# Sharing the low-rank turns of two head pairs, half-row residual products, and masks for the third and fourth pair in an attention and mixer kernel

## The chip, the cores and the metric

The kernel runs on one core of one Trainium2 chip. A core has TensorE (PE, matrix products, with its weight loads shown apart as PEld), VectorE (DVE), ScalarE (ACT), GpSimd (POOL) and SyncE (SP); POOL and SP issue the transfers here. The metric is the device time of one execution in microseconds. Before the change it is 213.51 us, the median of three runs (212.98 to 214.1).

## The reference

Two stages follow each other. The first is an attention over 4 batches, 8 heads, 768 positions and 64 channels, in which a query sees the 96 positions up to its own and the 8 first positions of the sequence, with a bias that falls with the distance. The second is a mixer whose input is the attention's output with the heads side by side (768 x 512 for each batch): a low-rank product along the positions (rank 32), added to its input, and a two-layer network along the channels (512 to 2048 to 512), added again.

```python
scores = scale * np.matmul(q, k.transpose(0, 1, 3, 2))
bias = -slopes[:, None, None] * dist[None, :, :]
scores = scores + bias[None, :, :, :]
scores = np.where(keep, scores, -1000000000.0)
a = np.exp(scores - max);  a = a / (np.sum(a, axis=-1, keepdims=True) + 1e-09)
x = (a @ v) with the heads side by side
h = xt @ U @ V                       # xt: x with positions last; U 768 x 32, V 32 x 768
u = x + h.transpose(0, 2, 1)
ch = np.maximum(u @ w_ch1, 0.0) @ w_ch2
return (u + ch).astype(np.float32)
```

## The kernel before, in words

Work is cut into named tasks. A task names its engine, its instructions, the tasks that it waits for and the buffers that it takes and gives back. A written list, `ORDER`, names all tasks in one order; the class `Planner` walks through it, gives each task a buffer and a planned start from written costs, and sorts the tasks by planned start. Each engine runs its tasks strictly in the order that results. So an instruction can stand behind another of its engine that still waits, although its own inputs are there. Waits themselves are inserted from the data that instructions read and write.

The 8 heads of a batch are taken as 4 pairs, so there are 16 pairs, numbered 0 to 15; a task's number is its pair's, or its batch's in the mixer. One pair goes through these tasks (function `attention`):

- loads of q, k and v (`lq`, `lk`, `lv`, issued by POOL); `TQ` and `TK` turn q and k on PE and `EQ`, `EK` copy the result out of PSUM (pairs 0 to 7), or a transposing transfer on SP does it (pairs 8 to 15); `KO` and `VC`, `VG` are copies of k and v in which the first keys stand in for others.
- `S`: scores on PE in three parts, with 64 rows of the array for each head. `EX`: exponent on ACT. For pairs in `CFG["BI"]`, the distance bias is put into PSUM ahead of the scores by products with a scaled identity (`SB`, line 754). For all others the exponent is multiplied by a mask on DVE (`MK`, lines 847 and 851); the masks come from ACT (line 1391).
- `PV`: weighted sums of v on PE (lines 906, 907). `RC`, `NM`: DVE divides by the sums and writes x in float32 (lines 941, 945). `XC` casts x to 16 bits. For pair 3, the last of batch 0, this runs in three pieces (`PV3.*`, `RC3.*`, `NH3.*`; `NH` writes 16 bits at once, line 925), and `NM3` writes the float32 copy apart.
- The low-rank part. `UP` (line 890): 32 columns, x times U. `XE` (line 996): a copy of them to SBUF, four times side by side. `XU` (line 999): one 128 x 128 product that turns this. `TE` (line 1012): a copy of the turned block to `tmp`, 128 columns for each pair. `HM` (line 1019): products of 32 rows of `tmp` with V, which give the low-rank term of that pair. From pair 4 on, two pairs share one `HM` with four products. `E0`, `E1` make uT, the mixer's input with channels on the partitions: a copy out of PSUM for pairs 0 to 3, where x is turned by identity products in the same banks, or an addition to a turned x which a transposing transfer (`XT`) has brought.

The mixer (function `mlp`) of a batch has a first layer on PE (`M1`, lines 1102 and 1126, and `ZP`, line 1196, a form with seven products in place of eight) with its evacuations on ACT and DVE, and a second layer (`P1` to `P7`, line 1318) in three row tiles. The first thing in each row tile is `RS` (line 1301): four products of 32 rows by 256 columns which put the low-rank term of the output into two banks. It reads `tmp` and `td`, the difference of the halves of `tmp`. DVE adds each finished bank to x in SBUF (`DA` to `DH`), and SP stores the rows (`O`).

Batches overlap: while PE works on the mixer of one, the attention of the next runs in the same lists. Ahead of the first mixer product of batch 0 (`M1a0.*`) stand the attention of pairs 0 to 3 and some of the turns of the next pairs. Where the planner sees PE idle before that, function `idle` puts in products with zeros.

PE takes 128 rows at once in most products, two groups of 64 rows in `S`, and groups of 32 rows in `HM` and `RS`; the code calls these modes 0, 1 and 2.

Of the kernel before, what the change touches and what calls it, by code (L numbers as in the profile page):

```python
# [21 lines left out]
lk0 lq0 wz lq3 ones2 iota Ck0.0 relf bias0 bias1 rel3 Ck0.1 Cq0.1 Cq0.0 TK0 SB0.2 TQ0 SB0.0 mask1 mask6 EQ0.0 EK0.0  # L22
EK0.1 KO0.1 KO0.0 SB0.1 ones1 lk1 TQ3 lq1 ones0 lk3 EQ0.1 S0.1 bias2 bias4 lv0 TK1 S0.0 EX0.1 EQ3 EK1 TQ1 S0.2 EQ1
SB1.1 KO1 TK3 EX0.0 EX0.2 vs1 EK3 SB1.0 VC0 VG0 lk2 lq2 S1.1 EX1.1 S1.0 EX1.0 ones3 lv1 KO3 u16 SB3.1 PV0 RC0 NM0 XC0
lv3 mask4 SB1.2 S1.2 vs0 EX1.2 S3.1 SB3.0 TK2 TQ2 EX3.1 VC1 VG1 EK2 SB3.2 S3.0 EQ2 lv2 EX3.0 VC3 VG3 KO2 S3.2 PV1 RC1
SB2.0 SB2.1 NM1 VC2 EX3.2 S2.1 S2.0 mask0 XC1 EX2.1 PV3.0 PV3.1 PV3.2 EX2.0 RC3.0 SB2.2 RC3.2 S2.2 VG2 NH3.0 UP0 NH3.2
EX2.2 RC3.1 UP1 XE0 XU0 PV2 NM3 NH3.1 RC2 back w1_3 XE1 XU1 TE0 HM0 UP3.0 UP3.1 UP3.2 NM2 XC2 lk4 TE1 HM1 w1_0 lk5 lq4
TK4 TK5 E00 mask3 E01 UP2 M1a0.0 XE3 EK4 XU3 XE2 TE3 TQ4 XU2 TE2 HM3 HM2 KO4 EK5 EQ4 E13 E03 M1c0.0 w1_1 lq6 E02 S4.1
M1a0.1 M1d0.0 M1c0.1 M1d0.1 EX4.1 EX4.2 MK4.1 MK4.2 KO5 mixl vs2 M1b0.0 RL0.0 M1a0.2 M1b0.1 RL0.1 M1b0.6 RM0.6 mask2
M1a0.7 M1c0.2 M1d0.2 M1b0.2 M1a0.6 lq5 TQ5 RL0.7 w1_2 RL0.2 mask5 M1a0.5 lv4 lk6 RL0.6 lv5 VC4 VG4 EQ5 M1b0.7 w1_6  # L30
w1_5 lk7 S4.0 RL0.5 RM0.7 S5.1 w1_4 EX4.0 TK6 M1a0.4 EX5.1 EX5.2 w1_7 M1a0.3 M1c0.3 M1d0.3 M1b0.3 EK6 TQ6 MK4.0 M1b0.5
RL0.4 RM0.5 RL0.3 lq7 ZS1 PV4 MK5.2 w2_1 w2_3 M1b0.4 KO6 RC4 w2_0 M1a0.10 EQ6 NM4 RM0.4 VC5 mask7 S6.0 S5.0 EX6.0
EX5.0 Sa0.0 TD0 Sc0.0 MK5.1 MK5.0 TK7 M1a0.11 M1b0.8 RL0.10 RL0.11 RM0.8 S6.1 EX6.2 M1a0.15 M1a0.14 M1b0.13 M1a0.8
M1b0.10 EK7 EX6.1 XC4 VG5 MK6.1 RL0.15 RL0.8 PV5 M1a0.13 RL0.13 Sb0.0 Sd0.0 M1a0.9 M1a0.12 RL0.14 M1b0.12 KO7 RC5
RL0.9 RM0.10 TQ7 M1b0.15 MK6.2 TWa1 NM5 RL0.12 RM0.12 RM0.13 M1b0.11 EQ7 RM0.11 TWb1 M1b0.14 M1b0.9 RM0.15 S7.1 RM0.14
RM0.9 RS0.0 RS0.2 P10.0 Sa0.1 Sb0.1 EX7.1 EX7.2 P10.2 MK7.1 Sd0.1 S7.0 RS0.1 lq8 w2_2 P20.1 TWa0 DA0.0 lv7 P30.1 DF0.1
MK6.0 MK7.2 TWb0 P10.1 P30.0 P50.1 P20.0 EX7.0 lk8 lv6 lv8 lv9 VC6 Sc0.1 DA0.2 MK7.0 DF0.0 EQ8 VG6 XC5 PV6 EK8 RC6 XT4
UP4 P60.0 P60.2 XE4 VC7 XU4 XT5 P50.2 UP5 lv10 VG7 VC8 XE5 NM6 XC6 KO8 TE4 P20.2 DB0.2 DC0.2 DC0.1 DA0.1 PV7 XU5 RC7
DB0.0 P30.2 UP6 NM7 P50.0 XC7 S8.0 P60.1 P70.0 DF0.2 XE6 EX8.0 TE5 ZS2 HM5 VC10 XU6 TE6 P70.2 DB0.1 UP7 DC0.0 P70.1
E04 DD0.2 E05 DD0.0 lk9 VG10 lk11 lk10 XE7 XU7 TE7 P40.2 HM7 P40.0 XT6 VC9 DD0.1 DG0.2 E06 XT7 DG0.0 ZP11.5 P40.1 E07  # L40
S8.1 E17 M1a1.1 ZT1 EX8.1 EX8.2 ZU1.5 M1b1.1 ZP11.4 RL1.1 M1a1.4 ZP51.4 ZU1.4 RL1.4 M1b1.4 ZP61.5 ZP11.6 ZU1.6 MK8.1
ZS3 ZP61.4 ZP21.6 DG0.1 MK8.0 ZP21.4 ZA1.6 ZP11.7 ZP61.6 RM1.4 ZW1.4 ZA1.4 lq10 lq11 VG9 EK9 KO9 ZP21.5 ZP71.4 ZX1.4
ZW1.6 ZA1.5 ZB1.4 M1b1.5 lq9 ZP51.6 ZP51.5 RM1.5 ZP71.6 ZU1.7 EK10 O0.3 O0.5 ZP31.4 ZX1.6 ZD1.4 ZP21.7 EK11 ZB1.6
ZP61.7 ZP41.6 ZA1.7 ZP41.4 ZP11.2 VG8 O0.1 O0.0 O0.2 ZW1.5 ZP71.5 ZP31.6 O0.4 ZR1.6 EQ9 EQ10 KO11 ZP21.2 KO10 MK8.2
ZU1.2 ZW1.7 ZD1.6 EQ11 ZA1.2 ZP51.7 ZP71.7 ZP61.2 ZR1.4 PV8 ZX1.5 ZP41.5 ZP11.3 ZX1.7 ZB1.5 ZP41.7 ZB1.7 ZP31.7 ZR1.5
RC8 NM8 XC8 lv11 ZP21.3 ZP31.5 ZD1.7 ZW1.2 ZU1.3 S9.0 ZP61.3 ZR1.7 ZP71.2 EX9.0 ZA1.3 ZD1.5 Sa1.1 ZW1.3 ZX1.2 M1a1.5
lk13 lq12 lk12 lv13 RL1.5 lk15 MK9.0 S9.1 ZP51.2 ZP71.3 ZP41.2 Sb1.1 ZP51.3 EX9.2 ZX1.3 ZB1.2 MK9.2 EX9.1 ZB1.3 M1a1.0
M1b1.0 RL1.0 ZR1.2 MK9.1 TD1 ZP31.2 ZP41.3 ZD1.2 ZR1.3 ZP31.3 EK12 PV9 ZD1.3 S11.1 RC9 EX11.1 NM9 RS1.2 P21.2 EX11.2
P11.2 S10.1 RS1.0 EX10.1 EX10.2 P21.0 P11.0 XC9 Sa1.0 XT8 XT9 EQ12 lk14 S10.0 S11.0 EX11.0 Sb1.0 Sd1.1 MK11.2 MK11.1
lq13 DA1.2 EX10.0 VC11 DA1.0 Sd1.0 P61.2 P51.2 P31.2 UP9 UP8 XE8 XE9 MK10.1 P61.0 MK10.2 Sc1.0 MK11.0 XU9 XU8 MK10.0  # L50
P31.0 TE9 DF1.2 DB1.2 DC1.2 PV10 RC10 TE8 VG11 DF1.0 PV11 RC11 NM11 P51.0 NM10 XC11 DB1.0 Sc1.1 XC10 KO12 lv12 RS1.1
P21.1 P51.1 HM9 P31.1 P11.1 E09 lq14 P71.2 lv14 E08 DC1.0 S12.1 DD1.2 P71.0 EX12.1 DC1.1 DF1.1 XT10 DD1.0 DA1.1 MK12.1
P41.2 UP10 UP11 EX12.2 DG1.2 P41.0 XE11 XU11 XE10 XU10 TE11 DG1.0 XT11 TE10 P61.1 HM11 S12.0 DB1.1 EX12.0 VC12 E010
# [18 lines left out]
ZR3.5 ZD3.3 ZP33.5 ZR3.4 ZD3.4 M1b3.5 RM3.5 ZR3.3 ZD3.5 Sa3.3 Sa3.0 Sb3.0 Sa3.1 RS3.0 RS3.1 RS3.2 P13.1 P13.2 P13.0
P23.1 Sd3.0 Sc3.3 Sa3.2 P23.2 DA3.1 P53.2 P53.1 Sb3.3 Sb3.2 DA3.2 Sd3.3 P23.0 Sb3.1 P63.1 P63.2 Sd3.1 Sd3.2 P33.1
Sc3.0 DF3.2 O2.4 DA3.0 Sc3.1 DC3.1 Sc3.2 DC3.2 DB3.1 P63.0 P53.0 DB3.0 DB3.2 P33.0 DC3.0 DF3.0 P73.1 P73.2 DD3.2 DD3.1
O2.3 DF3.1 P73.0 O3.2a DD3.0 P43.2b O2.1 O2.5 O3.0 P43.1 O3.5a O2.0 DG3.2b DG3.1 P43.0 DG3.0 P43.2a O3.1 O3.5c DG3.2a
O3.4 O3.3 O3.5b P33.2 DH3.2 O3.2
# [64 lines left out]
class Planner:  # L141
# [58 lines left out]
    def run(self, names):  # L200
# [5 lines left out]
        mode = 0  # L206
# [1250 lines left out]
```

## Time and profile before

| | us |
|---|---|
| median of three runs | 213.51 |
| the profiled execution, whole | 213.38 |
| its span, first to last instruction | 211.6 |
| around the span | 1.8 |
| PE busy | 204.1 |
| DVE busy | 178.8 |
| ACT busy | 134.1 |
| POOL busy | 74.8 |

PE's busy time is a sum of products that overlap each other, with modelled ends. How long a task holds PE is therefore read from the start of its first product to the start of the next task's first product, in the view of instructions in order of time. For DVE and ACT the durations can be taken as they stand; on DVE an instruction begins up to 0.1 us ahead of the end of the one before it.

### The profile page before, as it was taken

Reading aid. Unit: us, or ns where it says so; the run is one execution under the profiler, and the core shown is the slowest. Engines: PE = TensorE matmul, PEld = TensorE weight load, DVE = VectorE, ACT = ScalarE, POOL = GpSimd, SP = SyncE. Lnnn points to the kernel's source line nnn. Section 1 sums busy time; section 2 is a strip of 40 time slices with the busy share of each in tenths; the row PEclk is TensorE's granted clock in tenths of the full one; section 3 lists DMA queues with packets and bytes.
Section 4 is the critical chain, followed back from the end, with each engine's and each line's share of the span. In section 5 each row is a group of like instructions: output and inputs, shape, how many; then the busy total and the mean of one; then the engine's idle time right before and its main releaser. Section 6 shows DMA issues by size and latency. Waiting matters only on the chain.

```text
span 211.6 us, 5568 instructions
## 1 busy us (share of the span) xinstructions
PE 204.1 (96%) x2240; PEld 146.4 (69%) x2240; DVE 178.8 (85%) x361; ACT 134.1 (63%) x249; POOL 74.8 (35%) x99
## 2 busy tenths in 40 slices
PE   6999899999999999999999999999999999999993
PEld 2555656666699775566797866666879765668892
DVE  4889964989899989899999997859899987677982
ACT  5999799997846638788864465987362347760000
POOL 8997999754008910029466000042000000000000
PEclk9999999999999999999999999999999999999999
DMA  6999999999999999949999977429421302000335
GB/s 185 184 165 168 160 175 177 185 206 192 159 158 101 142 138 274 224 79 133 142 119 167 156 227 170 116 19 120 108 47 50 77 0 99 3 2 3 120 131 196
DMA packets 105545, 27.91 MB, mean 132 GB/s; under 512 B 93104, under 2 KB 102640, under 8 KB 105520
## 3 DMA queue, kind: packets, MB, share of 16 engines
q0 software_dynamic: 72976, 13.78, 82.2%
q1 hardware_dynamic: 32544, 13.78, 31.1%
q8 instruction: 17, 0.28, 0.6%
q14 instruction: 8, 0.07, 0.1%
HBM read 27.75 MB, written 6.29 MB: 161 GB/s over the span
## 4 chain that ended last, share of the span: by engine, by line
PE 78%; DVE 8%; DMA 7%; POOL 4%; issue 1%; ACT 1%; POOLq 0%; DVEq 0%
PE ps L1318 31%; PE ps L1196 18%; PE ps L1102 10%; PE ps L1126 6%; PE ps L773 4%; DMA uT<-x 3%; DMA vt<-in_v_dram 3%; PE ps L907 2%; DVE x_sb L945 2%; PE ps L906 2%; PE ps L1301 2%; POOL stgq L500 1%; PE ps L644 1%; POOL stgk L500 1%; POOL vt L508 1%
## 5 line engine op out<-in xcount | busy, mean ns | idle before, releaser
L838 ACT ACTIVATE ep<-ps 128x1024 f16<-128x1024 f32 (+1 forms) x48 | 43.6, 954 | 14.6 <-PE ps L773 14.3
L1318 PEld LDWEIGHTS <-htr 128*128 128x128 f16 x392 | 36.1, 98 | 6.3 <-issue 2.0
L1330 DVE TENSOR_TENSOR x_sb<-x_sb,ps 128x256 f32<-128x256 f32 (+1 forms) x60 | 26.6, 463 | 4.6 <-PE ps L1318 4.3
L1318 PEld LDWEIGHTS <-sA 128*128 128x128 f16 x288 | 27.1, 98 | 3.5 <-issue 0.2
L1102 PE MATMUL ps<-uT,w 128*128 128x384 f16 x144 | 27.0, 326 | 0.0
L1213 DVE CUSTOM_DVE_ANT_0 htr<-ps,zu 128x384 f16<-128x384 f32 x42 | 21.7, 553 | 6.1 <-PE ps L1196 5.2
L1318 PE MATMUL ps<-w,sA 128*128 128x256 f16 x192 | 24.1, 273 | 0.0
L1318 PE MATMUL ps<-tB,htr 128*128 128x256 f16 (+1 forms) x200 | 23.7, 268 | 0.0
L1318 PE MATMUL ps<-w,htr 128*128 128x256 f16 x192 | 23.6, 273 | 0.0
L409 ACT ACTIVATE zu<-ps 128x384 f32<-128x384 f32 x42 | 19.7, 490 | 5.8 <-PE ps L1196 3.8
L508 POOL DMA_DIRECT2D vt<-in_v_dram x16 | 16.7, 1045 | 15.5 <-ACT xus L409 10.8
L504 POOL DMA_DIRECT2D stgk<-in_k_dram x24 | 19.9, 852 | 5.6 <-DMA kT<-stgk 4.6
L504 POOL DMA_DIRECT2D stgq<-in_q_dram x24 | 19.9, 861 | 0.7 <-PE ps L644 0.4
L1196 PEld LDWEIGHTS <-w 128*128 128x128 f16 x144 | 13.8, 98 | 8.9 <-issue 0.3
L1102 PEld LDWEIGHTS <-w 128*128 128x128 f16 x144 | 13.7, 98 | 8.4
L1108 ACT ACTIVATE htr<-ps 128x384 f16<-128x384 f32 x36 | 16.6, 498 | 3.4 <-PE ps L1102 2.9
L851 DVE TENSOR_TENSOR ep<-ep,mask 128x1024 f16<-128x1024 f16 x24 | 16.1, 682 | 2.4 <-ACT ep L838 2.4
L970 POOL DMA_DIRECT2D x<-x_sb x2 | 1.7, 826 | 44.7 <-PE ps L1102 26.0
L1196 PE MATMUL ps<-uT,w 128*128 128x384 f16 x72 | 16.4, 326 | 0.1
L1196 PE MATMUL ps<-zt,w 128*128 128x384 f16 x72 | 16.5, 326 | 0.0
L945 DVE TENSOR_TENSOR x_sb<-ps,rcp 128x768 f32<-128x768 f32 x16 | 15.1, 951 | 0.6 <-DMA kO<-kT 0.3
L1126 PE MATMUL ps<-uT,w 128*128 128x384 f16 x80 | 15.0, 326 | 0.2 <-DVE uT L1052 0.2
(122 smaller groups left out, 404.1 us busy)
## 6 DMA issues: line engine op xcount, KB each, us to landing
out_dram<-x_sb SPq DMA_DIRECT2D x22, 256.0 KB, 2.3
vt<-in_v_dram POOLq DMA_DIRECT2D x16, 192.0 KB, 5.9
stgk<-in_k_dram POOLq DMA_DIRECT2D x24, 96.0 KB, 5.2
stgq<-in_q_dram POOLq DMA_DIRECT2D x24, 96.0 KB, 5.6
w<-in_moe_w_ch_dram POOLq DMA_DIRECT2D x8, 256.0 KB, 6.5
w<-in_moe_w_ch_dram POOLq DMA_DIRECT2D x4, 512.0 KB, 11.0
stgq<-in_q_dram POOLq DMA_DIRECT2D x3, 192.0 KB, 5.0
stgk<-in_k_dram POOLq DMA_DIRECT2D x3, 192.0 KB, 4.8
```

Source lines behind the costliest of these rows:

```text
L409: nc.scalar.activation(dst, src, AF.Copy)
L504: nc.gpsimd.dma_start(o[:, i], src[b, h0 + i].rearrange("(n p) d -> p n d", p=P))
L508: nc.gpsimd.dma_start(vt[gv.slot][:, :, :, 0:D], v[b, h0:h0 + 2].rearrange("h (n p) d -> p h n d", p=P),)
L838: nc.scalar.activation(ep[gep.slot][:, :, lo:512], ps[:, gsc.slot:gsc.slot + 2, lo:512], AF.Exp, scale=qk_scale)
L945: nc.vector.tensor_tensor(xo, pvo()[:, :, :, 0:D], rcp[p % 2].unsqueeze(3).broadcast_to((P, 2, NB, D)), ALU.mult)
L1102: nc.tensor.matmul(ps[:, g.slot, 0:HS], w1[:, dc, jt * P:(jt + 1) * P], ub[:, dc, i * HS:(i + 1) * HS], start=(dc == 0), stop=(dc == NDC - 1),
L1108: nc.scalar.activation(htr[:, jt, i * HS:(i + 1) * HS], ps[:, g.slot, 0:HS], AF.Relu)
L1126: nc.tensor.matmul(ps[:, g.slot + half, 0:HS], w1[:, dc, jt * P:(jt + 1) * P], ub[:, dc, half * HS:(half + 1) * HS], start=(dc == flat[0]) ...
L1196: nc.tensor.matmul(bank(g), a()[:, i], bq[:, i], start=first and i == 0, stop=last and i == 1, skip_group_check=True,)
L1213: return lambda: nc.vector._custom_dve(TENSOR_ADD_SAT, out=o, in0=x(), in1=y(), s0=3.0e38, s1=0.0)
L1318: nc.tensor.matmul(o if part is None else o[:, part], a[:, j, c0 + cols.start:c0 + cols.stop], bq[:, j] if part is None else bq[:, j, part ...
L1330: nc.vector.tensor_tensor(o, o, x, ALU.add)
```

## The change

Three things change, and the written order and the engines of several copies with them.

1. Two pairs of a batch share one low-rank turn. `UP` of the even pair writes 32 columns and that of the odd pair the next 32 of one bank. One `XE` copies the 64 columns twice side by side, one `XU` turns them and one `TE` copies the result out; `tmp` has 256 columns for a batch in place of 512. One `HM` with four products serves both pairs, in batch 0 too. So there are 8 each of `XE`, `XU`, `TE`, `HM` in place of 16, 16, 16 and 10. Both pairs' `UP` must be done ahead of them.
2. `RS` becomes eight products of 64 rows by 128 columns. Since the 64 rows of `tmp` hold both pairs, V stands in two copies with zeros in the other pair's rows: a fill with zeros (`vz`), and two differences and two copies in `vs2` in place of one difference. `td` is 128 columns wide in place of 256. `RS` has the mode of `S`.
3. Pairs 2 and 3 have no `SB`; their exponents are multiplied by masks (`MK2.*`, `MK3.*`). Six `SB` go, four scaled identities are not made, and six DVE products come.

In the new order the pairs of batch 0 are taken as 0, 1, 2, 3 (before: 0, 1, 3, 2), and the loads follow that. `EQ3` goes from DVE to ACT, `NM3` goes behind `NH3`, `TQ5` goes ahead of the first mixer product. That product is now `M1a0.3` (before: `M1a0.0`), and on PE it stands behind `UP2`, `UP3.*`, `TK5` and `XU3`. The order of the built program has 44 products with zeros ahead of the first mixer product in five places, besides the 8 at the start. The number of masks, loads and stores is the same; of the copies of k and v, `KO` goes by transfers on SP for 2 pairs in place of 3, and `VC` with `VG` for 1 pair in place of 3; ACT and DVE make the others. The last task on PE is `P43.0` (before: `P33.2`), and the last store is `O3.3`, 256 KB, which waits for `DG3.0` (before: `O3.2`, 128 KB, which waits for `DH3.2`).

```diff
-    "BI": [0, 1, 2, 3],
+    "BI": (0, 1),
-    "H2": [4, 6, 8, 10, 12, 14],
-    "R2": {0: (), 1: (), 2: (), 3: ()},
...
-    tmp = sb("tmp", [P, DM], FP16, 2)
+    tmp = sb("tmp", [P, 2 * P], FP16, 2)
-    td = sb("td", [P, hd], FP16)
+    td = sb("td", [P, P], FP16)
...
+    c_vz = add(DVE, 0.55, lambda: nc.vector.memset(vs[:, 1:3], 0.0), name="vz")
...
-                nc.vector.tensor_tensor(o, vf[:, 0:HS], vf[:, HS:S], ALU.subtract)
+                    nc.vector.tensor_tensor(vs[r, 1 + i], vf[r, 0:HS], vf[r, HS:S], ALU.subtract)
+                    nc.vector.tensor_copy(vs[r2, 1 + i], vs[r2, 0])
...
                     nc.tensor.matmul(
-                        low(0, R), xx[:, c], u16[:, c],
-                        start=turned and c == 0, stop=(c == NB - 1), skip_group_check=True,
+                        low(k * R, (k + 1) * R), xx[:, c], u16[:, c],
+                        start=leads and c == 0, stop=(c == NB - 1), skip_group_check=True,
                     )
...
+            def xuevac():
+                copy(
+                    ENG[CFG["XE"][p]], xus[gxu.slot].rearrange("p (g x) r -> p g (x r)", g=2),
+                    low(0, 2 * R).unsqueeze(1).broadcast_to((P, 2, 2 * R)),
+                )
...
+            XE = add(ENG[CFG["XE"][p]], 0.28, xuevac, [f_[-1], l_[-1]], acq=[gxu], name=f"XE{p}")
+            XU = add(PE, 0.06, xuturn, [XE], lat=0.3, rel=[gxu], name=f"XU{p}")
...
+            def hboth():
+                other()
+                hmix()
...
-            nc.vector.tensor_tensor(td, tb[:, hd:DM], tb[:, 0:hd], ALU.subtract)
+            nc.vector.tensor_tensor(td, tb[:, P:2 * P], tb[:, 0:P], ALU.subtract)
...
-                    for n, g, m in ((1, gX, td if i else tb[:, 0:hd]), (2, gY, tb[:, i * hd:(i + 1) * hd])):
-                        r = slice(VR[n] + k * R, VR[n] + (k + 1) * R)
-                        yield half(g, i), vs[r, n, cols], m[r], i == 0
+                    for k in range(2):
+                        for r, g, m in ((slice(64, P), gX, td if i else tb[:, 0:P]), (slice(0, 64), gY, tb[:, i * P:(i + 1) * P])):
+                            nc.tensor.matmul(
+                                half(g, i)[:, k * P:(k + 1) * P], vs[r, 1 + k, cols], m[r], start=i == 0 and k == 0, stop=False, skip_group_check=True,
+                            )
+            RS = add(PE, 0.23, rest, [TD] + mm1_done[b][-1:] + c_vs, lat=0.3, acq=[gX, gY], mode=1, name=f"RS{b}.{t}")
```

More of the change, by code (lines that the diff above doesn't have):

```diff
@@ L21 @@
 ORDER = """
[L22 to L41, printed above, removed]
@@ L72 @@
[L72 to L76, printed above, removed]
+wz lk0 lq0 lk1 iota relf rel3 bias1 bias0 bias2 Ck0.0 mask5 mask7 Ck0.1 Cq0.1 Cq0.0 TK0 lq1 SB0.2 lk2 ones1 EK0.0
@@ new lines @@
+EK0.1 vz ones0 TQ0 SB0.0 lv0 KO0.1 KO0.0 EQ0.1 SB0.1 EQ0.0 mask6 lq2 TK1 S0.0 S0.1 TQ1 EK1 KO1 EQ1 VC0 EX0.0 EX0.1 vs0
+S0.2 SB1.1 TK2 SB1.2 S1.1 S1.2 lv1 TQ2 EK2 ones2 EX0.2 mask4 EX1.2 lk3 lq3 ones3 u16 lv2 VG0 EX1.1 SB1.0 S1.0 KO2 EQ2
+PV0 S2.2 EX1.0 VC1 TK3 VG1 S2.1 lq5 w1_1 EX2.2 lv3 vs1 PV1 lk4 RC0 TQ3 w1_6 NM0 XC0 MK2.2 lk5 w1_0 EK3 EX2.1 RC1 S2.0
+KO3 EQ3 EX2.0 NM1 MK2.1 S3.0 S3.2 VC2 MK2.0 VG2 S3.1 EX3.0 UP0 TQ5 XC1 EX3.1 PV2 MK3.0 MK3.1 VC3 EX3.2 EQ5 UP1 XE1 XU1
+mask0 back TE1 HM1 MK3.2 E00 RC2 VG3 E01 NM2 PV3.0 XC2 PV3.1 PV3.2 RC3.1 RC3.0 RC3.2 NH3.0 NH3.1 mixl TK4 UP2 UP3.0
@@ new lines @@
+NH3.2 EK4 NM3 UP3.1 UP3.2 TK5 lk6 w1_5 lq4 w1_7 XE3 XU3 TE3 EK5 M1a0.3 KO5 w1_4 w2_2 lk7 lv4 w1_3 HM3 M1a0.2 M1c0.2
+M1c0.3 E13 E02 w2_0 mask1 E03 KO4 M1a0.1 M1c0.1 M1d0.2 S5.0 M1d0.3 M1b0.2 mask2 EX5.0 M1d0.1 M1b0.3 M1b0.1 M1b0.13
+M1a0.12 RL0.2 lv5 RL0.3 RL0.1 mask3 S5.1 lq6 M1a0.11 M1b0.14 EX5.1 w1_2 lq7 M1a0.13 TQ4 EX5.2 RM0.14 RL0.11 TK6 w2_1
+w2_3 RM0.13 RL0.12 RL0.13 MK5.1 MK5.2 EQ4 EK6 M1b0.12 RM0.12 M1a0.14 RL0.14 M1b0.10 S4.1 RM0.10 S4.0 M1b0.11 EX4.0
+M1a0.8 RM0.11 EX4.2 M1b0.15 M1a0.9 EX4.1 RL0.8 M1a0.15 M1a0.0 vs2 TK7 ZS2 MK4.2 TD0 EK7 MK5.0 MK4.0 VC4 MK4.1 M1a0.10
@@ L77 @@
+DF3.2 Sd3.1 P63.2 DA3.0 Sd3.3 P33.2 P53.0 P33.1 DC3.1 DB3.1 DC3.2 DH3.2 DB3.2 O3.2a O2.3 O2.2 DF3.1 DC3.0 O2.0 O2.5
+O3.1 O2.4 O2.1 P73.2 P73.1 P63.0 DD3.2 DD3.1 DB3.0 P33.0 P43.1 P43.2a P73.0 DF3.0 DG3.1 DG3.2a DD3.0 P43.2b DG3.2b
+O3.5a O3.0 O3.2 O3.4 O3.5b O3.5c P43.0 DG3.0 O3.3
 """.split()
@@ L206, in run @@
         mode = 0
-        dma_free = {POOL: 0.0, SP: 0.0}
+        dma_free = {POOL: 0.0}
         shared_port = {POOL: [], DVE: []}
@@ L276, in run @@
                 if t.eng == SP:
-                    behind = max(0.0, dma_free[POOL] - s - 0.8)
-                    begin = max(s + t.lead, dma_free[SP])
-                    dma_free[POOL] = max(dma_free[POOL], begin) + need
-                    dma_free[SP] = begin + need
-                    t.end = begin + need + min(0.7 * behind, 6.0) + (1.1 if late else 0.3)
+                    behind = max(0.0, dma_free[POOL] - s)
+                    dma_free[POOL] = max(dma_free[POOL], s + t.lead - 0.8) + need
+                    t.end = s + t.lead + min(0.8 * behind, 6.5) + (0.4 if late else 0.1)
                     clock[SP] += min(0.08 * behind, 0.6)
@@ L583 @@
             add(
-                POOL if vq else DVE, 1.1 if vq else 0.55, build_vs(g), [] if vq else [c_mixl],
+                POOL if vq else DVE, 1.1 if vq else 1.5, build_vs(g), [] if vq else [c_mixl, c_vz, c_vs[1]],
                 size=0.3 if vq else 0.0, parts=2 if vq else 1, fast=0, name=f"vs{g}",
@@ L608 @@
     nm_done, waiting, later = {}, {}, {}
-    m2_done, kept, zt_read, plain_mm, rs_done, rs_of = {}, {}, [], {}, {}, {}
+    m2_done, kept, zt_read, plain_mm, rs_done, ups, shared = {}, {}, [], {}, {}, {}, {}
     def attention(p):
@@ L978, in attention @@
             UP = add(
-                PE, 0.16 if turned else 0.49, mixed(range(NB)), [XC, c_u16], lat=0.3, acq=[gu], rel=[gx16],
+                PE, 0.16 if turned else 0.49, mixed(range(NB)), [XC, c_u16], lat=0.3, acq=[gu] if turned else [gu, gx], rel=[gx16],
                 name=f"UP{p}",
@@ L1009, in attention, with hmix @@
             XT = []
-        def tevac():
-            copy(ENG[CFG["TE"][p]], tmp[b % 2][:, hp * P:(hp + 1) * P], low(P, 2 * P))
-        TE = add(ENG[CFG["TE"][p]], 0.29 if CFG["TE"][p] == "D" else 0.3, tevac, [UP] + xw, rel=[gu] if turned else [], name=f"TE{p}")
-        def hmix(k=0, gx=gx):
+        def hmix(gx=gx):
             for half in (0, 1):
@@ L1057, in evacs, with low_copy, low_add @@
                 ut_done[p] = tuple(ee)
+            elif p in CFG["EA"]:
+                gh = Group("zu")
+                def low_copy():
+                    nc.scalar.activation(
+                        zu[gh.slot].bitcast(FP16).rearrange("p (h c) -> p h c", h=2), ps[:, gx.slot:gx.slot + 2, 0:HS], AF.Copy
+                    )
+                def low_add():
+                    o = uT[b % 2][:, hp]
+                    nc.vector.tensor_tensor(o, o, zu[gh.slot].bitcast(FP16), ALU.add)
+                AH = add(ACT, 0.81, low_copy, [HM], acq=[gh], rel=[gx], name=f"AH{p}")
+                ut_done[p] = (add(DVE, 0.555, low_add, [AH] + w + XT, rel=[gh], fast=2, name=f"E0{p}"),)
             else:
@@ L1068, in evacs @@
                 ut_done[p] = (add(e, 0.81 if e == ACT else 0.95, ev, [HM] + w + XT, rel=[gx], name=f"E0{p}"),)
-        if duo and p % 2 == 0:
+        if k == 0:
             later[p] = evacs
         else:
-            if duo:
-                later[p - 1](HM)
+            later[p - 1](HM)
             evacs(HM)
```

188 lines of the change are left out of this document (90 added, 98 removed).

## The prediction

> **What bounds the kernel now.** I read the page's head first, then the chain of work that ended last in order of time, then two stretches of the view of stages.
>
> ```profile
> span 211.6 us, 5568 instructions
> PE 204.1 (96%) x2240; PEld 146.4 (69%) x2240; DVE 178.8 (85%) x361; ACT 134.1 (63%) x249; POOL 74.8 (35%) x99
> PE   6999899999999999999999999999999999999993
> ```
>
> ```profile
> 17.41 0.34 DVE vo L411
> ...
> 24.59 1.01 DVE x L411
> ...
> 26.29 0.33 PE ps L1126 x2
> ...
> 38.81 0.34 PE ps L644 x6
> ...
> 57.28 0.32 PE ps L1301 x4
> ...
> 70.74 7.29 DMA uT<-x
> ...
> 189.13 0.54 PE ps L1301 x12
> 189.68 18.48 PE ps L1318 x176
> 208.18 0.42 DVE x_sb L1330
> ```
>
> ```profile
> 2.60:25.60 23.00, 20.21 (x343) 12.73 (x341) 20.50 (x54) 20.10 (x35) 21.75 (x31) 1.00 1.79 185
> 26.10:208.20 182.10, 181.73 (x1888) 132.59 (x1884) 157.47 (x307) 112.61 (x213) 50.89 (x60) 1.00 1.08 126
> ```
>
> The columns of the last two rows are the stretch, PE, PEld, DVE, ACT and POOL busy, clock, transfers. The chain has two parts with different limits. From 17.4 us to the cast of pair 2's x, which ends at 24.59 + 1.01 = 25.6 us, it runs on DVE. The first main product (first layer, batch 0) follows at 26.3 us. From there to 208.2 us PE is busy for 181.7 of 182.1 us. The chain leaves PE for a transfer at 70.74 us, but PE has other products meanwhile. So the end is the start of the first main product, plus PE's work behind it, plus the tail: last addition and store, 211.6 - 208.2 = 3.4 us. What the change saves on PE ahead of 26.3 us counts only if that start comes earlier; what it saves behind counts in full while PE isn't made to wait.
>
> **The early part.** PE loses six bias tasks; DVE gains six mask products.
>
> ```profile
> 12.08 0.60 PE L754 MATMUL ps<-rel,ibe 128*128 128x512 f16 x2
> 12.52 0.23 PE L907 MATMUL ps<-vt,ep 128*128 128x65 f16 x2
> ...
> 80.28 0.81 PE L1102 MATMUL ps<-uT,w 128*128 128x384 f16 x4
> 80.93 0.49 PE L1196 MATMUL ps<-zt,w 128*128 128x384 f16 x2
> ```
>
> ```profile
> L851 DVE TENSOR_TENSOR ep<-ep,mask 128x1024 f16<-128x1024 f16 x24 | 16.1, 682 | 2.4 <-ACT ep L838 2.4
> L847 DVE TENSOR_TENSOR ep<-ep,mask 128x768 f16<-128x768 f16 x12 | 6.5, 552 | 1.9 <-ACT ep L838 1.9
> L411 DVE COPY vo<-vt 128x660 f16<-128x660 f16 x7 | 2.9, 413 | 0.4 <-DMA vt<-in_v_dram 0.4
> ```
>
> ```profile
> 6.66 0.56 DVE L411 COPY qT<-ps 128x384 f16<-128x384 f16 x1 [0.60 <-PE ps L644]
> ...
> 7.95 0.96 DVE L411 COPY qT<-ps 128x768 f16<-128x768 f16 x1 [0.29 <-PE ps L625]
> ...
> 13.39 0.23 DVE L941 RECIPROCAL rcp<-ps 128x12 f32<-128x12 f32 x1 [0.95 <-PE ps L907]
> ...
> 21.98 0.25 DVE L411 CAST xus<-ps 128x128 f16<-128x128 f32 x1
> 22.16 0.93 DVE L945 TENSOR_TENSOR x_sb<-ps,rcp 128x768 f32<-128x768 f32 x1
> ```
>
> Two bias products of 512 columns hold PE for 12.52 - 12.08 = 0.44 us, and four of 384 columns take 0.65, so two 0.33. PE is rid of 4 x 0.44 + 2 x 0.33 = 2.4 us.
>
> On DVE, four masks of 682 ns and two of 552 ns come: 3.83 us. Away go `EQ3` (0.96, the row at 7.95, now on ACT), `XE0` (0.25, at 21.98) and, behind the needed pieces, `NM3` (0.93, at 22.16): 2.14 us. The fill `vz` has no row of its shape; it lies between 0 and the 0.41 us of the 660-wide copy. I take 0, since it stands where DVE waited 0.60 us for the first turned q; without that wait it would cost the 0.4. Net: +1.7 us of DVE work ahead of the last piece that PE needs, now `NH3.2`.
>
> DVE was busy for 20.5 of 23.0 us there, so 2.5 us were waits. If the new list fills all of them, `NH3.2` ends at 25.6 + 1.7 - 2.5 = 24.8 us; if none, at 27.3. I take the middle: the waits for first turns (0.60 and 0.29) hang on loads that come no earlier, and the smaller ones stay. The 0.95 us for pair 0's weighted sums is filled, because copies of pair 2 (`EK2`, `KO2`, `EQ2`) now stand before that reciprocal. 25.6 + 1.7 - 0.95 = 26.3 us. Before, the first main product came 0.7 us behind the cast; now `XE3` and `XU3` stand between as well (0.25 and 0.06), but fewer `UP` products are left: 0.8 us. So 27.1 in place of 26.3: **+0.8 us** (bounds -0.7 and +1.8).
>
> **Behind the first main product.**
>
> ```profile
> 53.99 0.23 PE L773 MATMUL ps<-qT,kO 64*128 64x128 f16 x2
> 54.06 0.22 PE L773 MATMUL ps<-qT,kT 64*128 64x128 f16 x2
> ...
> 65.35 0.22 PE L999 MATMUL ps<-ident,xus 128*128 128x128 f16 x1
> 65.41 1.04 PE L1318 MATMUL ps<-w,sA 128*128 128x256 f16 x8
> 66.28 0.30 PE L890 MATMUL ps<-u,x 128*128 128x32 f16 x6
> ...
> 69.05 1.03 PE L1318 MATMUL ps<-w,sA 128*128 128x256 f16 x8
> 70.02 0.23 PE L773 MATMUL ps<-qT,kT 64*128 64x128 f16 x2
> ...
> 72.14 0.34 PE L1019 MATMUL ps<-vs,tmp 32*128 32x384 f16 x4
> 72.42 0.23 PE L999 MATMUL ps<-ident,xus 128*128 128x128 f16 x1
> ```
>
> - `XU`: 65.41 - 65.35 = 0.06 us each; seven of the eight that go stand here: -0.4.
> - Mode changes: the same eight products take 0.87 us ahead of a 128-row product (65.41 to 66.28) and 0.97 ahead of a 64-row one (69.05 to 70.02), so a change costs 0.1. PE's order has 63 behind the first main product before and 59 after, since 9 of the 12 `RS` now stand beside scores of their own mode: -0.4.
> - `HM`: one with four products holds PE for 0.28 us with a change, 0.17 without. `HM2` and `HM3` were two; their products become four that run side by side: -0.17.
> - `RS`: alone 0.32 us with a change, 0.22 without; the three of the last batch took 0.54 together. Two products of 64 rows by 128 columns go every 0.06 us in the scores (53.99 to 54.06), so eight take 0.24 us. 12 x 0.24 against 9 x 0.22 + 0.44: about +0.4. If the two halves didn't run side by side it would be twice 0.24, +2.9 more; the scores speak against it.
> - `TQ5`, 0.34 us (the row at 38.81), is done ahead: -0.34.
>
> Together **-0.9 us**. At nothing I cost: 7 copies to `xus` and 7 to `tmp` less on ACT, busy for 134 of 211.6 us; the two more differences and the two copies of `vs2`, which lie while PE has first-layer products (cover gone: about 1 us); three fewer SP copies; the narrower `td`.
>
> **The tail.**
>
> ```profile
> out_dram<-x_sb SPq DMA_DIRECT2D x22, 256.0 KB, 2.3
> ...
> out_dram<-x_sb SPq DMA_DIRECT2D x3, 128.0 KB, 1.7
> ```
>
> The last store is now 256 KB in place of 128: +0.6 us. And `P43.0` waits for `DD3.0`, which waits for `P73.0`: 0.17 us until the end of a product is out (1.04 against 0.87 above) and 0.42 of addition, against half a product task (0.44) between them: +0.2. Together **+0.8 us**, with bounds 0 and 1.
>
> **Sum.** 0.8 - 0.9 + 0.8 = +0.7 us on the profiled execution's own 213.38 us (span 211.6 and 1.8 around it): 214.1 us. That execution lies 0.13 us under the median, well inside the runs' spread, so I leave 214.1 us. About 0.5% (1.1 us) is what a measurement of this kernel can tell from no change, so this is no change: 212.4 to 214.6 us.
>
> **The rivals.**
>
> *PE bounds the early part too (faster).* Then its start moves with its work: -2.4 - 0.9 + 0.8 = -2.5, 210.9 us. For it: PE is busy for 20.2 of 23 us there. Against it: the chain lies on DVE, and the new order holds 44 products with zeros there, places that have no work for PE. 0.08. A milder form is likelier: DVE's waits are all filled (-0.7) and the tail costs nothing, -1.6: 211.8 us, 0.14.
>
> *DVE becomes the bound outright (slower).* The masks stand in DVE's line ahead of `XC1`, `NM2`, `XC2` and `NH3`; a mask that waits for its exponent on ACT, busy 20.1 of 23 us there, holds all of these, and so `UP3` and the first main product. None of the 2.5 us filled gives +1.8 - 0.9 + 0.8 = +1.7, 215.1 us; one exponent late by 1 us more, 216.1. It decides once `NH3.2` ends later than 26.7 us. 0.28, at 215.3 us.
>
> *A shared turn comes too late in a later batch (slower).* The even pair's turn now waits for the odd pair. Where the chain runs through the transfer at 70.74 us, there was nothing to spare; 1.5 us there gives 215.6. Against it: PE has second-layer products to go on with. 0.06.
>
> *The half-row products don't do what is said:* 214.1 + 2.9 = 217.0 us; 0.02.
>
> *The masks hold up the loads (slower).*
>
> ```profile
> 29.59 1.53 POOL L554 DMA_DIRECT2D w<-in_moe_w_ch_dram  x2
> ...
> 29.64 0.69 DVE L851 TENSOR_TENSOR ep<-ep,mask 128x1024 f16<-128x1024 f16 x1 [1.56 <-ACT ep L838]
> ...
> L554 POOL DMA_DIRECT2D w<-in_moe_w_ch_dram x8 | 6.2, 793 | 0.7 <-DMA u<-in_moe_U_dram 0.7
> ```
>
> POOL issues nearly all loads early. If each mask kept POOL from issuing for its length, v of pair 3 would come 3.8 us later: 217 us. But two issues took 1.53 us while a mask ran, and eight have a mean of 793 ns, so none was held: 0.02. [...]
>
> **How the numbers follow.** Forecast, no change: 0.40, at 214.1 us. Faster: 0.08 + 0.14 = 0.22. Slower: 0.28 + 0.06 + 0.02 + 0.02 = 0.38. The range goes from 211.7 us, just under the milder faster case, to 216.1, the late exponent; about 0.1 lies beyond each end. The forecast's own range is 212.4 to 214.6.
>
> **What would show it.** The first main product at 27.1 us; `NH3.2` at 26.3; DVE without a wait near 0.95 us around 13 us; PE's stretch from that product to its last one 181.0 us in place of 181.9; a wait of about 0.2 us ahead of the last product task; the last store landing 0.6 us later behind its addition. It is wrong if the first main product comes before 25.9 or after 27.6 us, or if PE waits for over 1 us in sum between 30 and 200 us for a copy of uT.

## The result

The first four executions of the changed kernel gave 214.63, 214.71, 216.94 and 221.67 us, beside 213.26 us for the kernel before in the same session: a ratio of 1.010 (95% interval 1.0061 to 1.0138). Twelve more, among the experiments below, gave 213.87 us in the median (212.6 to 217.5) against 213.23 us: a ratio of 1.0023 (0.9999 to 1.0047). Over all sixteen the middle is 214.2 us; the prediction was 214.1. So by the larger set the change makes no difference that can be measured, and by the first four it is slower by 1%. The spread between executions is itself a result: 35 executions of the kernel before in that last session lay between 212.54 and 214.27 us. The ratios leave out executions over 1.5% above a kernel's fastest, of which the changed kernel has several and the kernel before next to none.

The profiled execution took 214.63 us (before: 213.38), with a span of 212.9 (211.6). The head of its page:

```profile
span 212.9 us, 5699 instructions
PE 205.9 (97%) x2312; PEld 149.6 (70%) x2312; DVE 181.6 (85%) x368; ACT 133.6 (63%) x241; POOL 75.0 (35%) x99
```

The chain that ended last, in order of time, around the first main product and at the end (start, length, engine, tile and line):

```profile
24.36 0.87 DVE x_sb L946
25.23 0.02 issue
25.25 0.94 DVE x L408
26.19 0.05 issue
26.24 0.23 PE ps L887
...
28.21 0.23 PE ps L1020
28.44 0.42 PE ps L1140 x2
...
207.56 0.43 DVE x_sb L1328
207.99 0.04 issue
208.03 1.05 PE ps L1316 x8
209.08 0.02 issue
209.11 0.42 DVE x_sb L1328
```

The first main product (line 1140) comes at 28.44 us, 2.15 later than before. DVE's last addition begins at 209.11 in place of 208.18. From one to the other it is 180.67 us in place of 181.89, so 1.22 us are won there. From the last addition's start to the end of the span it is 3.75 us in place of 3.42, so 0.33 are lost. 2.15 - 1.22 + 0.33 = 1.26 us, which is the difference of the spans (1.3 as printed). The chain begins a piece where the one before it ends; the first main product itself starts at 28.37 us here and at 26.14 before, and below these starts are given. The view of stages for the same two stretches (columns as before):

```profile
2.60:27.45 24.85, 22.78 (x382) 15.56 (x380) 22.27 (x59) 20.83 (x34) 22.42 (x33) 1.00 1.69 178
28.40:209.10 180.70, 180.52 (x1917) 132.78 (x1915) 157.90 (x308) 111.24 (x205) 50.07 (x59) 1.00 1.05 124
```

Behind the first main product PE is still never idle for long (180.52 of 180.70 us). So the question is the 2.15 us ahead of it. The first turn of k shows where they begin. In the view of instructions in order of time, before and after:

```profile
5.13 0.49 PE L644 MATMUL ps<-ident,stgk 128*128 128x128 f16 x6 [1.02 <-DVE stgk L411]
```

```profile
5.40 0.80 PE L643 MATMUL ps<-ident,stgk 128*128 128x128 f16 x6 [0.91 <-DVE stgk L408]
```

Six equal products took 0.49 us before and 0.80 after. The trace's records of the granted clock agree: the first record, of the full clock, begins at 3.58 us in the profile of before and at 8.83 us in that of after. (The views print a clock of 1.00 for a stretch ahead of the first record too; the slow products show that it wasn't.) A second profile of the same program, below, has the same row at the same time with the clock from 4.91 us:

```profile
5.40 0.49 PE L643 MATMUL ps<-ident,stgk 128*128 128x128 f16 x6 [0.92 <-DVE stgk L408]
```

DVE's waits up to 25.6 us in the first profile (sum, times, longest):

```profile
DVE kT L408 <- PE ps L624: 1.4, 1, 1.4
DVE stgq L408 <- DMA sA<-in_q_dram: 0.9, 1, 0.9
```

The first line is the wait for the turned k of pair 1, 0.7 us in the second profile: here DVE pays for the late turns. The second line is not the clock's work. Pair 0's q landed 4.9 us after its issue here, against 3.7 in the second profile. It is a rival for the late start, but PE was busy without a break from 5.42 to 8.83 us (3.41 of 3.41 us), so the turns waited for PE and not for that q.

### The profile page after: what moved, and what is told of

Its sections match the earlier page's. It is cut to its first block, busy times and chain, and to the rows that moved or that the text cites. A ratio compares the mean times of both kernels' runs of the same rounds, so it can differ in the third digit from the quotient of the medians.

```text
span 212.9 us, 5699 instructions
## 1 busy us (share of the span) xinstructions
PE 205.9 (97%) x2312; PEld 149.6 (70%) x2312; DVE 181.6 (85%) x368; ACT 133.6 (63%) x241; POOL 75.0 (35%) x99
## 4 chain that ended last, share of the span: by engine, by line
PE 87%; DVE 9%; issue 1%; POOL 1%; ACT 0%; POOLq 0%; DVEq 0%
PE ps L1316 35%; PE ps L1210 19%; PE ps L1116 11%; PE ps L1140 6%; PE ps L772 5%; PE ps L908 2%; PE ps L907 2%; PE ps L643 2%; PE ps L1305 1%; DVE x_sb L946 1%; DVE vo L408 1%; PE ps L753 1%; PE ps L891 1%; PE ps L1002 1%; DVE x L408 1%
## 5 line engine op out<-in xcount | busy, mean ns | idle before, releaser
L1328 DVE TENSOR_TENSOR x_sb<-x_sb,ps 128x256 f32<-128x256 f32 (+1 forms) x60 | 27.1, 462 | 4.9 <-PE ps L1316 4.2
L1116 PE MATMUL ps<-uT,w 128*128 128x384 f16 x144 | 26.2, 326 | 0.0
L850 DVE TENSOR_TENSOR ep<-ep,mask 128x1024 f16<-128x1024 f16 x28 | 18.9, 684 | 6.4 <-ACT ep L837 6.4
L1316 PE MATMUL ps<-tB,htr 128*128 128x256 f16 (+1 forms) x200 | 24.2, 268 | 0.1
L1210 PE MATMUL ps<-uT,w 128*128 128x384 f16 x72 | 16.0, 326 | 0.0
L1140 PE MATMUL ps<-uT,w 128*128 128x384 f16 x80 | 15.1, 326 | 0.0
```

The source lines that it names most:

```text
L850: nc.vector.tensor_tensor(ev, ev, mv, ALU.mult)
L1116: nc.tensor.matmul(ps[:, g.slot, 0:HS], w1[:, dc, jt * P:(jt + 1) * P], ub[:, dc, i * HS:(i + 1) * HS], start=(dc == 0), stop=(dc == NDC - 1),
L1140: nc.tensor.matmul(ps[:, g.slot + half, 0:HS], w1[:, dc, jt * P:(jt + 1) * P], ub[:, dc, half * HS:(half + 1) * HS], start=(dc == flat[0]) ...
L1210: nc.tensor.matmul(bank(g), a()[:, i], bq[:, i], start=first and i == 0, stop=last and i == 1, skip_group_check=True,)
L1316: nc.tensor.matmul(o if part is None else o[:, part], a[:, j, c0 + cols.start:c0 + cols.stop], bq[:, j] if part is None else bq[:, j, part ...
L1328: nc.vector.tensor_tensor(o, o, x, ALU.add)
```

## The experiments

Theory C: the late full clock makes the first turns late and so the first main product; its price is 1.2 us. Theory D, its rival: DVE's longer list, the 3.8 us of masks above all, sets the start whatever the clock does. (C, D, T and Q are only names for what an experiment sets out to tell apart.) Where nothing else is said, the kernels compute all that the reference does.

**More zeros at the start, and fewer**

```diff
 # after
-                    idle(int(gap / 0.43), 512, bank)
+                    idle(int(gap / 0.43) + 3, 512, bank)
```

> The changed kernel with 11 products with zeros at the start in place of 8. Theory C (clock at the start): in the changed kernel's profile PE stood without work from 4.5 to 5.4 us and its full clock was granted only at 8.8 us (before: 3.6), which moved every first turn and the first main product by 1.2 us. With PE busy until about 5.5 us the clock is granted by then, the first main product comes at 27.2 us in place of 28.4, and the time is 213.4 us. Rival D (DVE's list alone is late): the clock changes nothing that counts, first main product at 28.4 us, 214.6 us.

Measured: 214.72 us (ten executions), ratio 1.0057 (1.0039 to 1.0075). In its profile the full clock came at 6.40 us and the first main product at 27.37, 1.0 us earlier than in the profile of after; but the span was again 212.9. Neither theory had that. The gain was lost in one place, in the list of PE's waits between 150 and 160 us:

```profile
PE ps L772 <- DMA qT<-stgq: 0.9, 1, 0.9
```

These are the scores of pair 13 (`S13.1`), which wait for its turned q. They start at 154.40 us in both profiles; in that of after PE came there no earlier and found q ready. The load `lq13` is the last of three that POOL issues behind `XC12`, here at 143 us; the transposing transfer on SP waits for it.

The counterpart, on the kernel before:

```diff
 # before
-                    idle(int(gap / 0.43), 512, bank)
+                    idle(3, 512, bank)
```

> The kernel before with 3 products with zeros at the start in place of 8. Theory C: PE stands idle from about 2.1 to 5.1 us, the full clock comes only at about 8.5 us in every run, the first turns are later by 1.2 us and the time is 214.6 us. Rival (when the clock comes is chance and no matter of these products): within 0.3 us of the kernel before.

Measured: 214.33 us, ratio 1.0042 (1.0021 to 1.0064). The full clock came at 10.29 us, the first main product at 27.40 in place of 26.14, and the span was 212.7 in place of 211.6. So C's mechanism is real: in the kernel before, 6.7 us more without the full clock moved the first main product by 1.3 us and the span by 1.1.

**Bias products back**

```diff
 # after
-    "BI": (0, 1),
+    "BI": (0, 1, 2, 3),
 # ORDER: bias4 made behind bias2; SB2.*, SB3.* each ahead of its S; MK2.*, MK3.* out
 # each task's buffer held to that of after; the planner then sets 18 small zeros in place of 44
```

> The changed kernel with bias products for pairs 2 and 3 again (six SB in, six masks out), all else in its order and its PSUM banks. Theory D: DVE's line is the limit ahead of the first main product; 3.8 us of masks less bring it forward by 1.5 to 2 us although PE has 2.4 us more work, to about 26.5 us with an early clock and 27.5 with a late one; 212.7 to 213.7 us. Theory C alone: the masks cost nothing, PE has 2.4 us more to do, 214.6 us or more.

Measured: 214.38 us (213.81 to 217.6), ratio 1.0058 (1.0023 to 1.0093). The profiled execution got the full clock at 9.94 us and its first main product at 29.64. With eleven zeros besides:

```diff
 # after, with the bias products back as above
-                    idle(int(gap / 0.43), 512, bank)
+                    idle(int(gap / 0.43) + 3, 512, bank)
```

> The kernel after with TensorE's bias products back for pairs 2 and 3 (no masks for them) and with eleven zero products at the start in place of eight. If the late grant of the full clock makes the spread of the run with the bias products alone (213.8 to 216.3), the times should now stand together at 213.3 to 213.9 us. If the start of the first main product is set by DVE's list and not by the masks or the clock, 214.2 or more.

Measured: ratio 1.0074 (1.0041 to 1.0107); full clock at 5.83 us, first main product at 27.84. Eleven zeros did not hold the times together (214.03 to 218.32), so a late clock at the start is not shown to be what spreads them. D falls in this order of tasks: without the masks the first main product comes later, not earlier. The order was not made for bias products, so what they would cost in one of their own is not shown. Which engine is full is seen in the stages 5 to 10 and 10 to 25 us, of this kernel and then of the kernel after in its second profiled execution (below), where the full clock came at 4.91 us:

```profile
5.00:10.00 5.00, 5.00 (x70) 2.94 (x70) 3.60 (x10) 4.84 (x11) 5.00 (x10) 1.00 1.56 177
10.00:25.00 15.00, 14.32 (x262) 9.21 (x263) 11.17 (x25) 12.73 (x19) 14.99 (x19) 1.00 1.95 176
```

```profile
5.00:10.00 5.00, 4.60 (x78) 3.01 (x78) 3.95 (x12) 4.88 (x11) 5.00 (x10) 1.00 1.59 178
10.00:25.00 15.00, 13.91 (x297) 11.02 (x291) 14.62 (x35) 13.93 (x20) 15.00 (x19) 1.00 1.97 174
```

With bias products DVE has work for 11.17 of 15 us and PE for 14.32; with masks DVE for 14.62 and PE, zeros included, for 13.91.

**Only the masks, on the kernel before**

```diff
 # before
-    "BI": [0, 1, 2, 3],
+    "BI": [0, 1],
 # ORDER: SB2.*, SB3.*, bias4 out; masks made earlier on ACT; MK3.*, MK2.* behind their EX
```

> The kernel before with masks in place of bias products for pairs 2 and 3, and nothing else but the order of the eight masks on ACT. Theory D: 3.8 us more on DVE ahead of the first main product, of which about 1 to 2 us are hidden in its waits: first main product at 28 to 29 us, 215 to 216 us. Rival (PE bounds the early part): 2.4 us less on PE, 211 to 213.4 us.

Measured: 218.0 us, ratio 1.0208 (1.0173 to 1.0243), worse than both. The view of stages shows why; the third number from the end of a row is the granted clock:

```profile
18.00:21.33 3.33, 0.80 (x22) 0.63 (x23) 3.24 (x9) 2.33 (x4) 3.33 (x5) 1.00 1.97 173
21.33:24.74 3.41, 3.41 (x52) 3.12 (x48) 2.58 (x8) 0.81 (x2) 3.41 (x5) 0.50 1.96 159
```

PE stood mostly idle from 18 to 21.33 us (0.80 us of work), and for the next 3.41 us it got half the clock. Theory T: such a stretch follows whenever PE idles enough. To test it, zeros were put where PE had stood idle:

```diff
 # before with masks, as above
+            if t.name in ("S2.1", "PV3.0"):
+                bank = pl.unused("ps", t.start - 0.01, t.start)
+                idle(32 if t.name == "S2.1" else 16, P, bank)
```

> The kernel before with masks for pairs 2 and 3 (218.0 us, half clock from 21.33 to 24.74 us), and with 32 zero products of 128 columns ahead of S2.1 and 16 ahead of PV3.0, where TensorE stood idle for 2.2 and 1.2 us. Theory T: with TensorE busy there the clock stays full, the first main product comes at about 28.5 us in place of 30.5, and the time is 215 to 216.5 us. The rival: half clock as before, 218.

Measured: 216.59 us, and the clock stayed full:

```profile
18.00:21.33 3.33, 3.31 (x66) 3.12 (x64) 3.24 (x10) 2.19 (x4) 3.02 (x4) 1.00 1.94 174
21.33:24.74 3.41, 2.67 (x64) 2.38 (x60) 3.29 (x10) 1.74 (x3) 3.41 (x5) 1.00 1.82 133
```

The first main product came at 29.30 in place of 30.46 us. T holds here. What is left, 29.30 against 26.14, was not taken apart further: it is the masks together with an order that was not made for them.

**Without the 44 small zeros**

```diff
 # after
-                elif bank is not None and gap > 0.15:
+                elif False:
```

> The kernel after without the 44 zero products of 128 columns ahead of the first main product (the eight of 512 columns at the start stay). Theory T: idle TensorE in the early part makes the clock fall to half for a stretch of about 3.4 us, as in the run of before with the masks, at 21.3 to 24.7 us. Then such stretches come in most runs, and the time is 216 to 222 us with a mean granted clock of 0.984 to 0.992. The rival, that the grant depends on something else than TensorE's idle time: 214.6 us, as after.

Measured: 214.66 us (212.97 to 219.78), ratio 1.0056 (1.0019 to 1.0092). One execution in ten had a mean clock of 0.990, the others 0.995 to 1.0; with these zeros three of sixteen had 0.992 or less. So the strong form of T, that these zeros keep the clock up, falls. In the profile the full clock came at 3.89 us and the first main product at 25.82. But PE then waited 1.0 us for pair 13's q again, and 0.3 in another place; the span was 212.0.

**The load of pair 13's q, and the tail**

```diff
 # after, tail: ORDER
-P33.0 P43.1 P43.2a P73.0 ... P43.2b ... P43.0 DG3.0 O3.3
+P33.0 P73.0 ... P43.1 ... P43.0 ... DG3.0 P43.2a ... O3.3 P43.2b O3.5b DG3.2b O3.5c
```

> The kernel after with the last eight product tasks in another order: P73.0 two places earlier, P43.0 behind P43.1, and the two half tasks P43.2a and P43.2b last, so that the last store is 64 KB in place of 256 KB and P43.0 has another task between itself and P73.0. The theory that the tail costs 0.37 us for its larger last store and 0.16 us for the wait of P43.0: both are won back, and some of a smaller store still, 0.5 to 0.9 us under the kernel after, so 213.7 to 214.1 us where after's two even runs gave 214.63 and 214.71. The rival, that the store's landing time doesn't depend on its size there and the wait only moves: no difference, 214.6.

Measured: 214.91 us (212.4 to 217.6), ratio 1.0029 (1.0003 to 1.0054). In the profile the end lay 3.27 us behind PE's last product in place of 3.79, so 0.52 are won. The wait ahead of `P43.0` is gone too, but the last half task, `P43.2b`, now waits for the addition of the other half:

```profile
207.97 0.61 PE L1263 MATMUL ps<-tB,htr 128*128 128x128 f16 x8 [0.38 <-DVE x_sb L1294]
```

Read from start to start, `P43.0` came 0.23 us late in the kernel after and `P43.2b` comes 0.54 late here. That leaves a net gain of about 0.2 us, less than expected and too small to be seen in the times. This profile too lost 0.9 us to pair 13's q.

Theory Q: that load is what the earlier start runs into.

```diff
 # after with eleven zeros: ORDER
-XC12 lv13 ... lv15 ... lq13
+lq13 XC12 lv13 ... lv15
```

> The kernel after with eleven zero products at the start (as the run that gave 214.17 to 214.9 us and lost 0.9 us to the turned q of pair 13 at 154 us), and with the load lq13 issued ahead of XC12, lv13 and lv15 in POOL's line. Theory Q: with an early first main product, that q, whose load is the last of three issued together near 143 us, sets a new bound, and what the early part wins is lost there. Then no wait for it is left, and the time is 213.3 to 213.9 us. The rival, that another wait takes its place or the loads behind it come late instead: 214.2 to 214.9, as without it.

Measured: 213.11 us (ten executions, nine of them 212.6 to 214.24, one 217.47), ratio 0.9991 (0.9974 to 1.0009). Without the early load the same kernel had 1.0057 (1.0039 to 1.0075). PE had no listed wait between 30 and 205 us, and the span was 211.5. Theory Q holds.

> The same, with the last product tasks in the order that puts the two half tasks last (last store 64 KB). The two gains add if each is on the path: 212.7 to 213.4 us in undisturbed executions, about the time of the kernel before or 0.2% under it. If the tail's gain is a wait that only moves: 213.3 to 213.9.

Measured: 213.53 us (212.38 to 218.46), ratio 1.0000 (0.9982 to 1.0017), so the tail added nothing that could be seen in the times. Its chain shows the same wait of `P43.2b`, whose eight products start when the addition ahead of them has ended:

```profile
207.50 0.30 DVE x_sb L1294
207.80 0.04 issue
207.84 0.62 PE ps L1263 x8
208.46 0.02 issue
208.49 0.29 DVE x_sb L1294
```

The same with eight zeros at the start and without the small ones:

> The kernel after with lq13 early and the half tasks last, with eight zero products at the start and without the 44 small ones. From the run without the small ones (first main product at 25.8 us where the full clock came at 3.9 us; it lost 1.0 us to pair 13's q): 212.0 to 212.8 us where the clock comes early, 0.2 to 0.5% under the kernel before; where it comes late, 0.5 us more for each us of delay, up to 215.

Measured: ratio 1.0015 (0.9986 to 1.0043). The profiled execution took 211.98 us (span 210.1, full clock at 4.44 us, first main product at 25.59), the shortest of all; but the times spread from there to 217.0, so the median gains nothing. No version beat the kernel before by more than can be measured.

**The kernel after again**

> The kernel after, unchanged, timed in more executions. If the late grant of the full clock is a matter of chance from execution to execution, its times spread from about 213.4 us (early grant, less the wait for pair 13's q) to over 216; if it comes from the kernel, they stand near 214.7.

Measured: the 213.87 us and the ratio of 1.0023 given above. The times spread as for a matter of chance. The profiled execution, of 217.39 us, had the full clock at 4.91 us and its first main product at 26.67, 1.7 us earlier than in the other profile of the same program: with DVE's list the same in both, this decides against D as it was put. But it still ended 2.7 us later, so this long execution does not come from a late start. Its waits on DVE and on PE between 88 and 104 us, and its stages:

```profile
DVE x_sb L946 <- DMA out_dram<-x_sb: 3.3, 1, 3.3
```

```profile
PE ps L1116 <- DVE x_sb L946: 2.7, 1, 2.7
```

```profile
97.00:99.70 2.70, 0.04 (x1) 0.00 (x0) 0.99 (x2) 0.00 (x1) 2.70 (x4) 1.00 1.87 126
100.48:103.90 3.42, 3.42 (x19) 1.50 (x18) 1.84 (x4) 1.91 (x5) 3.42 (x6) 0.50 2.39 152
103.90:110.00 6.10, 6.10 (x92) 5.07 (x90) 6.07 (x8) 5.14 (x6) 2.77 (x4) 1.00 2.16 169
```

`NM9` must write x where the store `O0.3` still reads. That store stands in SP's line behind six transposing transfers and stores; `EK11` there went at 88.34 us, behind a load that POOL had issued at the same 78.79 us as in the other profile. So `O0.3` left at 93.97 (92.57 in the other profile) and landed 4.6 us later, `NM9` waited 3.3 us, all of DVE's list behind it waited too, PE ran dry at 97.0, and half the clock for 3.4 us followed. In all PE fell 4.5 us behind: from 1.7 ahead of the other profile to 2.75 behind it.

## Why the prediction was right, and where it was wrong

The start against the moment of the full clock, by the traces:

| kernel | full clock from, us | first main product, us |
|---|---|---|
| before | 3.58 | 26.14 |
| before, three zeros | 10.29 | 27.40 |
| after, second profile | 4.91 | 26.67 |
| after, tail | 5.01 | 26.61 |
| after, eleven zeros, lq13 early, tail | 6.82 | 27.45 |
| after, eleven zeros, lq13 early | 5.98 | 27.03 |
| after, eleven zeros | 6.40 | 27.37 |
| after | 8.83 | 28.37 |
| after, bias products back, eleven zeros | 5.83 | 27.84 |
| after, bias products back | 9.94 | 29.64 |
| after, no small zeros | 3.89 | 25.82 |
| after, no small zeros, lq13 early, tail | 4.44 | 25.59 |

- *The early part, +0.8 us (bounds -0.7 and +1.8).* In the first profile +2.15, outside the bounds and behind the 27.6 us that the prediction itself called wrong; in the second +0.53, inside. This is the step that failed: it has no term for the moment of the full clock. The table splits it. In the kernel after, each us of late clock costs (28.37 - 26.67) / (8.83 - 4.91) = 0.43 us; the four other rows with the 44 small zeros and the masks lie within 0.1 us of that line. In the kernel before it costs 0.19. Carried back to 3.58 us, which is earlier than any of these rows, after's line gives 26.1 us, the same as before. So by this estimate the change itself costs the start nothing, and the rest is 5.25 us of late clock. At a given clock, in this order, bias products instead of masks would be 0.8 us later (27.84 against 27.07 on the line at 5.83 us). The step counted the waits of DVE that the masks would fill, and that came true: the 0.95 us around 13 us is gone, and DVE works for 14.86 of the 15 us from 10 to 25, before 13.57. What it left out is that this slack had absorbed late first turns.
- *The stretch behind, -0.9 us.* Measured -1.22 with the new wait of 0.23 us ahead of `P43.0` inside, which the prediction counted in the tail; without it -1.45. So it was right in sign and too small by more than a third. `RS` holds PE for 3.56 us in all, before 3.24: +0.3 where +0.4 was said. `HM` of the later pairs holds 0.27 us as before, with half as many `XU` of 0.06. Mis-sized was the place just behind the first main product: before, `XU2`, `HM3` and `HM2` took 0.86 us there, waits included, after only one `HM3` of 0.27; -0.17 was said for the `HM`.
- *The tail, +0.8 us.* Measured 0.23 for the wait (0.2 was said), from start to start of products, and 0.33 for the store (0.6 was said).
- *DVE becomes the bound outright.* Half right: DVE is full from 10 us on (14.86 of 15 us in the first profile of after, 14.62 in the second). But a full DVE does not by itself make a late start: with the same masks and without the small zeros the first main product came at 25.6 to 25.8 us, ahead of the 26.14 before. `NH3.2`, at 27.45 us in the first profile, was at 25.75 in the second.
- *PE bounds the early part.* Its faster time was not reached, though the parts were there: where the clock came at 3.89 to 4.44 us and the small zeros were gone, the first main product came at 25.6 to 25.8 us. In the first of these two kernels pair 13's q then took back 1.0 us; in the second, with that load early and another tail, the one profiled execution took 211.98 us, near the 211.8 of this rival's milder form.
- *A shared turn too late.* Not seen; the late transfers that were seen are a q and a store.
- *Half-row products side by side.* Right. The first `RS` of batch 0 in the view in order of time, with what precedes and follows it:

```profile
55.05 0.22 PE L772 MATMUL ps<-qT,kT 64*128 64x128 f16 x2
55.11 0.33 PE L1305 MATMUL ps<-tmp,vs 64*128 64x128 f16 x5
...
55.43 0.72 PE L1316 MATMUL ps<-w,htr 128*128 128x256 f16 x5
```

55.43 - 55.11 = 0.32 us for eight products and the change of mode; the two of the last batch that stand ahead of others of their mode took 0.234 and 0.223, where 0.24 was said.
- *Masks hold up the loads.* Not seen: between 10 and 25 us POOL's issues took about as long in the first profile of after as before: 852 ns in the mean for k (839), 824 for q (855), 1024 for v (1043). In the second profile k's took 1033 ns, but 962 also with the bias products back.

The forecast of no change, 214.1 us, held on the middle of sixteen executions, and in part by luck: in the first profile each part was off, a late clock by chance against a larger gain behind. It did not see the two waits for transfers, at 97 and at 154 us, that take back an early start.

## What to carry to other kernels

When a change fills an engine's last waits, ask what those waits had absorbed: a chance at the start (here the clock) then costs twice as much (0.43 us for each us of late clock, before 0.19). Follow a gain to the end: earlier work meets transfers that come no earlier (pair 13's scores began at 154.40 us with the earlier start as without it), so look for the loads and stores with the least slack behind it; moving one load ahead was worth 0.7% here (1.0057 to 0.9991). One late store can cost more than all of the change, as in the execution of 217.39 us, where PE fell 4.5 us behind. Profile a second execution before trusting a difference of 1%.

## What was not expected of the hardware

- The moment of the full clock differed between two executions of one program: 8.83 and 4.91 us, with the same eight zeros from 0.89 us. Over all profiles it lay between 3.58 and 10.29 us.
- In three traces the changes of the clock lie whole multiples of 3.413 us apart: the record of the full clock lasts 61 times as long in the kernel before (208.21 us) and 60 times in the first profile of after (204.80), and from 4.91 to 100.48 us in the second profile of after it is 28 times. Each of the two stretches at half the clock shown above lasted 3.4 us (21.33 to 24.74 and 100.48 to 103.90).
- What decides when the full clock comes is not shown. In the 3.41 us just ahead of it PE was busy for 2.69 us in the kernel before (0.17 to 3.58) and for 3.41 in the first profile of after (5.42 to 8.83). The 3.42 us ahead of that, with 2.51 us of work (2.00 to 5.42), were not followed by the full clock.
- Ahead of each stretch at half the clock PE had had little to do: 0.04 us of work in the 2.70 from 97.00 to 99.70 us in the second profile of after, and 0.80 in the 3.33 from 18.00 to 21.33 in the kernel before with masks. With zeros put there, 3.31 us of work, the clock stayed full.
- Zeros on PE may not be free: without the 44 small ones the first main product came at 25.82 us at a full clock from 3.89, where the line of the kernel after, carried on, gives an estimate of 26.67 - 1.02 x 0.43 = 26.2, and at 25.59 from 4.44, where it gives 26.5. The times show no difference.
